# Four blocks of a position bias moved into the main run, and the first tokens' split moved apart from their transposition

## The chip, the cores and the metric

The kernel runs on one core of a Trainium2 chip. The metric is the device time of one execution in microseconds, as the median of several runs. The profile is one further execution, recorded by the hardware profiler.

## What is computed

Attention with a bias that a small MLP makes from positions, and then a mixture of experts (MoE) on the result. B = 8 batches, H = 8 heads, S = 576 positions, 64 columns a head; 4608 tokens of 512 columns, 8 experts, one expert for each token.

```python
scores = scale * np.matmul(q, k.transpose(0, 1, 3, 2))
x = (psi_rel / psi_i)[..., None]          # log1p(|i-j|) / log1p(max(i,1))
bias = np.maximum(x @ w1 + b1, 0.0) @ w2  # hidden 32, one value a head
scores = scores + bias.transpose(2, 0, 1)[None, :, :, :]
attn = softmax(scores); x = attn @ v      # tokens of 8 heads x 64
e_idx = np.argmax(x @ w_gate + modality_bias[modality_id], axis=1)
out[mask] = gate_w[mask, None] * (np.maximum(x[mask] @ w1[e], 0.0) @ w2[e])
```

## The kernel before, in words

The program has three stages. **The bias table** is made once. The 576 query rows are cut into 36 blocks of 16 rows. For each block four hidden tiles are made (L189 on ACT for the first of four, L191 on DVE for the others), TensorE multiplies them with w2 into a PSUM tile (`bias_out`, L199), and `bias_put` scales that into an output tile (L215 on ACT, L213 on DVE for the blocks in PUT_DVE) and issues its transfer on SP's queue. Blocks 0 to 31 are the main queries: each is one transfer of 288 KB into NBm (L218). NBm is read in four quarters, and quarter c holds blocks 8c to 8c + 7. Blocks 32 to 35 are the last 64 queries: each is four transfers of 72 KB into NBr (L223). `bias_table` runs blocks 0 to 31 in a loop with hooks for loads and transposes at given blocks; blocks 32 to 35 are generators (`bias_late`), which LATE steps at the head of the first units of pair 0: a first step makes the hidden tiles, a second the matmuls and the put.

**Attention** runs 32 pairs of heads, each in five units of queries: units 0 to 3 read the four quarters of NBm, unit 4 reads NBr. A unit is scores S (L400, TensorE), addition of the bias with row maximum (L414, DVE, `CUSTOM_DVE_ANT_0 Eb<-sps,NBm`), exponential (L429, ACT), transposes (L444), and the product with V (L486) three units later. ORDER writes the order of these steps by hand. In the following S(0,4) is the score step of pair 0's unit 4. A new pair's q, k, v come through SP's queue; V0 says where pair 0's V is loaded, (0, 1) being unit 1 of pair 0. Behind each transfer on SP the next waits in order; the transfers go round over eight semaphores, so that one is issued when the eighth before it has landed.

**MoE** runs tiles of 256 tokens. Weights and tokens are split into a high and a low part in fp32r: a cast on ACT makes the high part, a subtraction on DVE the low part (`wsplit` L1173, L1174; `wsplit_cols` L1181, L1182; tokens in `xprep`, L1195, L1196). `xprep` also copies gates and token numbers on POOL (L1190, L1191) and transposes the tokens on DVE (L1194). `phase1` multiplies with w1 (L1212), `phase2` with w2 (L1229), and `mo` (L1237) scales the result for the rows' transfer out. K = 5 tiles, the first ones, are dealt out from batches whose attention is done; `first_tiles` places the first tile's preparation among the last units of attention: the table `at` maps (place, unit) to what is done there.

Of the kernel before, what the change touches and what calls it, by code (L numbers as in the profile page):

```python
# [11 lines left out]
F32 = mybir.dt.float32  # L12
# [4 lines left out]
ALU = mybir.AluOpType  # L17
# [15 lines left out]
NDC = DM // P  # L33
NFC = F // P
TS = 256
# [5 lines left out]
NMAIN = P // 4  # L41
NBLK = S4 // 4
# [66 lines left out]
class Attn:  # L109
# [8 lines left out]

    ON_POOL, ON_DVE = (), (1,)


    LAG = 1
    PUT_DVE, ON_ACT2 = (21, 31, 34), ()
    TURN0, SPLIT0, QK1 = (4, 8), (6, 10), (9, 10, 11, 12, 13, 14, 15, 16)
    V0 = (0, 1)
    ROUTE = (6, 7, 8, 15, 16, 18)

    ROUTE_LATE = ((1, 1), (1, 2), (1, 3), (1, 4), (2, 0), (2, 1), (2, 3), (3, 0), (3, 1))  # L130

    LATE_HIDDEN = ((31, 0),)
    LATE = ((0, 1), (0, 0), (0, 2), (0, 1), (0, 3), (1, 2), (1, 3))

    def bias_setup(self):

# [43 lines left out]
    def bias_hidden(self, blk, cg, by):  # L180

        nc = self.nc
        s = bias_base(blk, cg)
        win = self.tg[:, X0 - s : X0 - s + S]
        c = self.shift[:, 4 * blk + cg : 4 * blk + cg + 1]
        h = next(h for h in self.bias_free if blk < NMAIN or not any(h is x for x in self.bias_main))
        self.bias_free = [x for x in self.bias_free if x is not h]
        if by == "act":
            nc.scalar.activation(h, win, AF.Relu, bias=c)  # L189
        else:  # L190
            (nc.gpsimd if by == "pool" else nc.vector).tensor_scalar(h, win, c, 0.0, op0=ALU.add, op1=ALU.max)  # L191
        return h
# [32 lines left out]
    def bias_table(self, hooks):  # L225

        ready = {}
        self.late = [self.bias_late(blk) for blk in range(NMAIN, NBLK)]

        def ahead(blk, cg):  # L230
            if blk < NMAIN and (blk, cg) not in ready:
                by = "pool" if cg == 3 and blk in self.ON_POOL else "act" if cg == 0 and blk not in self.ON_DVE or cg == 1 and blk in self.ON_ACT2 else "dve"
                ready[blk, cg] = self.bias_hidden(blk, cg, by)

        with self.tc.tile_pool(name="bps", bufs=3, space=PSUM) as pp:
            done = []
            for blk in range(NMAIN):
                ps = pp.tile([P, 1024], F32, tag="bps", name=f"bps{blk}")
                if blk + 3 in self.ON_POOL:
                    ahead(blk + 3, 3)  # L240
                for k in range(2):
                    if blk + k not in self.ON_DVE:
                        ahead(blk + k, 0)
                    if blk + k in self.ON_ACT2:
                        ahead(blk + k, 1)
                for cg in range(4):
                    ahead(blk, cg)
                    self.bias_out(cg, ready.pop((blk, cg)), (ps[:, 0:512], ps[:, 512:S]))
                for at, k in self.LATE_HIDDEN:
                    if at == blk:  # L250
                        next(self.late[k])
                if len(done) == self.LAG:
                    self.bias_put(*done.pop(0))
                done.append((blk, [(slice(0, S), ps[:, 0:S])]))
                for f in hooks.get(blk, ()):
                    f()
            for d in done:
                self.bias_put(*d)
# [299 lines left out]
    def attention(self):  # L558
        n_pair = self.n_pair
        tail = self.first_tiles() if self.K else {}  # L560
        for at in self.ROUTE_LATE:
            tail.setdefault(at, []).append(lambda: next(self.route, None))
        for u, k in self.LATE:
            tail.setdefault((0, u), []).append(lambda k=k: next(self.late[k], None))
        tail.setdefault(self.V0, []).append(lambda: self.load_v(0))
        bg = None
        for n in range(n_pair + 1):
            for u in range(5):
                for f in tail.get((n, u), ()):
                    f()  # L570
                if n == 1 and u == 0:
                    bg = self.blanks()
                if u == 4 and n > 0 and n % NP == 0:
                    assert not bg or all(k == len(x) for x, k in bg)
                    bg = self.route_steps(n // NP - 1)
                m, w = (n, u - 2) if u >= 2 else (n - 1, u + 3)
                scored = []
                for op in self.ORDER[u].split():
                    op, self.defer = op[0], int(op[1:] or 0)
                    if op in "aAbc":  # L580
                        self.flush(lambda x: x[0][0] in "er")
                    elif op == "X":
                        self.flush(lambda x: x[0][0] == "a")
                    self.held = [] if self.defer and op in "tTRAc" else None
                    if op in "SefC":
                        if n == n_pair:
                            continue
                        if op == "S":
                            scored = self.scores(n, u)
                        elif op == "C":  # L590
                            self.compact(n, u)
                        else:
                            self.exps(*scored["ef".index(op)])
                    elif op in "tT":
                        if 0 <= m < n_pair:
                            self.etrans(m, w, "tT".index(op))
                    elif op == "x":
                        if n > 0:
                            self.flush(lambda x: x[0][:2] == "av")
                            self.turn_x(n - 1)  # L600
                    elif op in "RaAbc":
                        if n > 0:
                            self.rtrans(n - 1) if op == "R" else self.av(n - 1, *divmod("aAbc".index(op), 2))
                    elif op in "qk01V":
                        if n + 1 < n_pair:
                            if op == "V":
                                self.load_v(n + 1)
                            elif op in "qk":
                                self.turn(n + 1, "qk".index(op))
                            else:  # L610
                                self.split(n + 1, int(op))
                    elif op == "L":
                        if n + 2 < n_pair:
                            self.load_qk(n + 2)
                    elif f := self.route_next(bg, "XB".index(op)):
                        f()
                    fresh, self.held = self.held or [], None
                    for x in self.waiting:
                        x[2] -= 1
                    self.flush(lambda x: x[2] <= 0)  # L620
                    self.waiting += fresh
                if 0 <= m < n_pair:
                    del self.E[m, w]
        self.flush(lambda x: True)
        self.bg = bg
# [555 lines left out]
        self.nc.scalar.copy(h, w)  # L1181
        self.nc.vector.tensor_tensor(l, w, h.bitcast(F32), op=ALU.subtract)  # L1182

    def xprep(self, t, x):

        nc = self.nc
        gx = self.gx[t % 2]
        for w in range(2):
            at = NDC * TS + 2 * w
            nc.gpsimd.tensor_copy(self.gate(t)[w], gx[:, at : at + 1])  # L1190
            nc.gpsimd.tensor_copy(self.ids_of(t)[w], gx[:, at + 1 : at + 2])  # L1191
        xh, xl = self.xh[t % 2], self.xl[t % 2]
        x = x.rearrange("p (c w) -> p c w", c=NDC)
        nc.vector.transpose(x, gx[:, 0 : NDC * TS].rearrange("p (a c i) -> p c a i", c=NDC, i=32))  # L1194
        nc.scalar.copy(xh, x)  # L1195
        nc.vector.tensor_tensor(xl, x, xh.bitcast(F32), op=ALU.subtract)  # L1196

    def phase1(self, t, before, beside):
        nc = self.nc
# [47 lines left out]
    def tile(self, t, beside=None, between=()):  # L1247

        parts = iter(range(NDC))
        beside = beside or (lambda: None)  # L1250
# [20 lines left out]
        self.load_new(t + 1, 1)  # L1271
        for c in range(NDC):
            self.wsplit(0, c)

        def middle(w):
            if w == 0 and t + 1 < self.T:
                self.xprep(t + 1, self.xt)
            beside()

        self.phase2(t, middle)  # L1280
        if t + 2 <= self.K:
            self.moe_rows(t + 2)
        if t + 2 <= self.T:
# [2 lines left out]
    def first_tiles(self):  # L1286

        nc = self.nc
        n = self.n_pair - NP
        at = {}  # L1290

        def add(pair, u, f):
            at.setdefault((n + pair, u), []).append(f)
# [5 lines left out]
        add(2, 4, lambda: self.load_rows(0))  # L1299
        for part, to in enumerate(((2, 4), (3, 1), (3, 3), (4, 0))):  # L1300
            add(*to, lambda part=part: self.load_part(1, part))
        add(4, 0, lambda: self.xprep(0, self.Eb[:, next(self.e_next)].rearrange("p h s -> p (h s)")[:, 0 : NDC * TS]))
        add(4, 3, lambda: self.wsplit_cols(0))
        return at

    def route_rest(self):
# [21 lines left out]
    def moe_rest(self, st):  # L1328
# [7 lines left out]
        if K == 0:  # L1336
            self.moe_load(0)
            self.load_new(0, 1)
            self.xprep(0, self.xt)
            self.moe_load(1)  # L1340
        first = self.sure - 2 * NT
        for t in range(K, self.sure):
# [150 lines left out]
```

## Time and profile before

| | us |
|---|---|
| median of 3 runs (1005.96 to 1006.64) | 1006.18 |
| the profiled execution's own time | 1007.5 |
| its span in the trace | 1005.4 |
| PE busy | 972.1 (97%) |
| DVE busy | 709.4 (71%) |
| ACT busy | 712.7 (71%) |
| POOL busy | 303.1 (30%) |

The span runs from the first to the last instruction that the trace holds; 2.1 us of the profiled time lie around it. PE is TensorE's matmul stream. The bias table takes the time to about 55 us, attention to about 573 us, MoE the rest. A row of a timeline gives its start, its duration (of a whole run of equal instructions where it ends in x2 or more), the engine, the line, and in square brackets how long the engine stood idle before it and which instruction released it.

### The profile page before, as it was taken

The page shows a single profiled execution, that of the slowest core. Times are in us where ns is not written, and L with a number is a line of the kernel's source. Part 1 is how long each engine was busy: PE and PEld are TensorE (multiplying, and loading weights), DVE is VectorE, ACT ScalarE, POOL GpSimd, SP SyncE. Part 2 cuts the span into 40 slices and gives each one's busy share as a digit, 9 for nine tenths or more (in the row PEclk, how much of TensorE's full clock was granted, in tenths as well). Part 3 has the DMA queues.
Part 4 walks back from the last instruction along what each step waited for, and adds up shares of the span by engine and source line. Part 5 has one row for each costly group of instructions (what it writes and reads, how often), then busy time and mean ns, then how long its engine had stood idle before and what let it go on. Part 6 is the DMA issues. An engine that isn't in the chain of part 4 may idle for free. (4 is left out here: it accounts for less than half of the span.)

```text
span 1005.4 us, 22478 instructions
## 1 busy us (share of the span) xinstructions
PE 972.1 (97%) x8110; PEld 762.4 (76%) x8110; DVE 709.4 (71%) x1441; ACT 712.7 (71%) x1366; POOL 303.1 (30%) x489
## 2 busy tenths in 40 slices
PE   7969999999999999999999899999999999999997
PEld 4547767767677676776667589889999998989896
DVE  8965768776777777777877677886666656565655
ACT  7977988888888888888888555455555555454554
POOL 1512433625426254262542513511111111111111
PEclk9998999999999999999999999999999999999999
DMA  6977755564655646546469430312117821162610
GB/s 163 194 166 152 196 104 116 109 131 101 128 108 105 134 100 120 119 101 133 94 121 212 128 112 32 96 48 64 43 43 190 271 64 54 61 195 68 186 43 24
DMA packets 327417, 116.34 MB, mean 116 GB/s; under 512 B 283247, under 2 KB 304111, under 8 KB 327299
## 3 DMA queue, kind: packets, MB, share of 16 engines
q1 hardware_dynamic: 321234, 95.80, 43.3%
q0 software_dynamic: 5920, 19.03, 5.4%
q8 instruction: 65, 1.06, 0.5%
q14 instruction: 54, 0.43, 0.2%
q10 hardware_dynamic: 144, 0.00, 0.0%
HBM read 144.34 MB, written 33.34 MB: 177 GB/s over the span
## 5 line engine op out<-in xcount | busy, mean ns | idle before, releaser
L414 DVE CUSTOM_DVE_ANT_0 Eb<-sps,NBm 128x576 f32<-128x576 f32 x256 | 183.6, 754 | 125.0 <-PE sps L400 57.1
L429 ACT ACTIVATE Eb<-Eb,mn 128x576 f32<-128x576 f32 x288 | 221.0, 769 | 13.6 <-DVE mn L414 12.6
L332 ACT ACTIVATE eT<-eps 128x512 f32<-128x512 f32 x256 | 148.9, 595 | 55.7 <-PE eps L444 54.8
L400 PE MATMUL sps<-QK 64*128 64x288 f32 (+1 forms) x1728 | 171.7, 310 | 7.5 <-DVE mn L414 7.0
L400 PEld LDWEIGHTS sps<-QK 64*128 64x128 f32 (+1 forms) x1728 | 134.3, 186 | 48.1 <-DVE mn L414 29.6
L1212 PE MATMUL p<-QK,w1hi 128*128 128x256 f32 x1136 | 161.8, 285 | 2.8 <-DVE QK L1196 2.2
L444 PE MATMUL eps<-idf,Eb 128*128 128x128 f32 x1024 | 149.6, 280 | 3.6 <-DVE eT L334 1.9
L1212 PEld LDWEIGHTS p<-QK,w1hi 128*128 128x128 f32 x1136 | 147.1, 191 | 7.3 <-DVE QK L1196 3.0
L486 PE MATMUL xps<-eT,vraw 128*64 128x288 f32 x1024 | 149.3, 416 | 0.0
L444 PEld LDWEIGHTS eps<-idf,Eb 128*128 128x128 f32 x1024 | 113.3, 141 | 37.5 <-issue 13.6
L1238 POOL DMA_INDIRECT out<-mo,idt x36 | 39.5, 1099 | 308.1 <-ACT mo L1237 252.4
L1214 ACT ACTIVATE hh<-p 128x512 fp32r<-128x512 f32 x72 | 43.1, 598 | 123.0 <-PE p L1212 116.7
L1215 DVE SCALAR_TENSOR_TENSOR hl<-p,hh 128x512 fp32r<-128x512 f32 x72 | 49.7, 691 | 101.6 <-ACT hh L1214 97.8
L1229 PE MATMUL p<-w2hi,hh 128*128 128x512 f32 x288 | 112.3, 390 | 0.0
L1229 PE MATMUL p<-w2hi,hl 128*128 128x512 f32 x288 | 112.3, 390 | 0.0
L434 POOL COPY rem<-Eb 128x128 f32<-128x128 f32 x128 | 37.0, 291 | 244.1 <-ACT Eb L429 238.3
L1174 DVE TENSOR_TENSOR w2lo<-NBm,w2hi 128x1024 fp32r<-128x1024 f32 x72 | 89.5, 1243 | 16.0 <-ACT w2hi L1173 15.7
L486 PEld LDWEIGHTS xps<-eT,vraw 128*64 128x64 f32 x1024 | 62.3, 136 | 39.9 <-issue 12.4
L1212 PE MATMUL p<-QK,w1lo 128*128 128x256 f32 x568 | 91.2, 283 | 0.0
L1174 DVE TENSOR_TENSOR w1lo<-NBm,w1hi 128x1024 fp32r<-128x1024 f32 x72 | 85.0, 1243 | 0.0
L1212 PEld LDWEIGHTS p<-QK,w1lo 128*128 128x128 f32 x568 | 78.3, 192 | 0.0
L1173 ACT CAST w2hi<-NBm 128x1024 fp32r<-128x1024 f32 x72 | 74.9, 1040 | 0.0
(219 smaller groups left out, 1451.0 us busy)
## 6 DMA issues: line engine op xcount, KB each, us to landing
NBm<-moe_w SPq DMA_DIRECT2D x84, 512.0 KB
NBm<-moe_w SPq DMA_DIRECT2D x42, 1024.0 KB
NBr<-xg SPq DMA_DIRECT2D x80, 128.0 KB
kraw<-k SPq DMA_DIRECT2D x128, 72.0 KB
xd<-xt SPq DMA_DIRECT2D x128, 72.0 KB
vraw<-v SPq DMA_DIRECT2D x64, 128.0 KB
NBm<-xTb SPq DMA_DIRECT2D x24, 288.0 KB
NBm<-moe_w SPq DMA_DIRECT2D x3, 2048.0 KB
```

Of the source, the lines that this page charges most:

```text
L332: self.nc.scalar.activation(out, ps, AF.Copy, scale=scale)
L400: nc.tensor.matmul(self.sps[h][:, half, 0:HS], QK[o, q, qs], QK[o, k, HS * half : HS * half + HS], start=i == 0, stop=i == 2, skip_group_c ...
L414: nc.vector.tensor_tensor_reduce(out=e.rearrange("p (t w) -> p t w", t=2), in0=self.sps[h][:, :, 0:HS], in1=nb.rearrange("p (t w) -> p t w ...
L429: self.nc.scalar.activation(e, e, AF.Exp, bias=mn, scale=-1.0, accum_out=sm)
L444: nc.tensor.transpose(ps[:, k, :], e[:, part, P * k : P * k + P], self.idf)
L486: nc.tensor.matmul(ps[out : out + 64, :], lhsT, rhs, tile_position=(row, out), skip_group_check=True, **kw)
L1173: self.nc.scalar.copy(h, w)
L1174: self.nc.vector.tensor_tensor(l, w, h.bitcast(F32), op=ALU.subtract)
L1212: nc.tensor.matmul(ps[:, a, :], w[:, c, fs], x[:, c, :], start=i == 0, stop=i == len(ops) - 1)
L1214: nc.scalar.activation(hh[:, sl, :], ps, AF.Relu)
L1215: nc.vector.scalar_tensor_tensor(hl[:, sl, :], ps, 0.0, hh[:, sl, :].bitcast(F32), op0=ALU.max, op1=ALU.subtract)
L1229: nc.tensor.matmul(ps, h[:, f, sl], m[:, f, :], start=i == 0, stop=i == len(ops) - 1)
```

## The change

Three things change. In the bias table, SEQ is the order of the main loop: the four blocks of the last 64 queries (32 to 35) stand in it behind main blocks 7, 11, 15 and 19, main blocks 29, 30 and 31 leave it, and the hooks go by place in SEQ. Blocks 29 to 31 are the late ones; LATE steps them behind the scores of units 0 and 1 instead of ahead of them. Their puts are on DVE (29 and 31) and ACT (30), and main block 21's stays on DVE. For the first tile, `xprep` is cut into `xturn` (POOL copies, transpose) and `xsplit` (cast, subtraction); `xturn` stays at (4, 0), `xsplit` goes to (4, 2), and the split of the first w1 columns moves from (4, 3) to (4, 2) behind it. In each later tile `xturn` stands between the second and the third part of the w1 split, and `xsplit` behind the fourth, ahead of phase 2; before, all of `xprep` stood behind the first half of phase 2.

```diff
-    PUT_DVE, ON_ACT2 = (21, 31, 34), ()
+    PUT_DVE = (21, 29, 31)
-    LATE_HIDDEN = ((31, 0),)
-    LATE = ((0, 1), (0, 0), (0, 2), (0, 1), (0, 3), (1, 2), (1, 3))
+    SEQ = (*range(8), 32, *range(8, 12), 33, *range(12, 16), 34, *range(16, 20), 35, *range(20, 29))
+    LATE = ((0, 0), (0, 1), (0, 2), (1, 1), (1, 2))
...
-        self.late = [self.bias_late(blk) for blk in range(NMAIN, NBLK)]
+        self.late_blocks = [blk for blk in range(NBLK) if blk not in seq]
+        self.late = [self.bias_late(blk) for blk in self.late_blocks]
...
-            for blk in range(NMAIN):
+            for at, blk in enumerate(seq):
...
-                for at, k in self.LATE_HIDDEN:
-                    if at == blk:
-                        next(self.late[k])
+                if at == len(seq) - 1:
+                    next(self.late[0])
...
-                for f in hooks.get(blk, ()):
+                for f in hooks.get(at, ()):
...
-        for u, k in self.LATE:
-            tail.setdefault((0, u), []).append(lambda k=k: next(self.late[k], None))
...
                             scored = self.scores(n, u)
+                            for _, j in (x for x in self.LATE if (n, x[0]) == (0, u)):
+                                next(self.late[j], None)
...
-    def xprep(self, t, x):
+    def xturn(self, t, x):
...
+        return x
+
+    def xsplit(self, t, x):
+
+        xh, xl = self.xh[t % 2], self.xl[t % 2]
+        self.nc.scalar.copy(xh, x)
+        self.nc.vector.tensor_tensor(xl, x, xh.bitcast(F32), op=ALU.subtract)
...
             self.wsplit(0, c)
-
-        def middle(w):
-            if w == 0 and t + 1 < self.T:
-                self.xprep(t + 1, self.xt)
-            beside()
-
-        self.phase2(t, middle)
+            if c == 1 and t + 1 < self.T:
+                x = self.xturn(t + 1, self.xt)
+        if t + 1 < self.T:
+            self.xsplit(t + 1, x)
+        self.phase2(t, lambda w: beside())
...
-        add(4, 0, lambda: self.xprep(0, self.Eb[:, next(self.e_next)].rearrange("p h s -> p (h s)")[:, 0 : NDC * TS]))
-        add(4, 3, lambda: self.wsplit_cols(0))
+        x0 = []
+        add(4, 0, lambda: x0.append(self.xturn(0, self.Eb[:, next(self.e_next)].rearrange("p h s -> p (h s)")[:, 0 : NDC * TS])))
+        add(4, 2, lambda: self.xsplit(0, x0[0]))
+        add(4, 2, lambda: self.wsplit_cols(0))
```

On SP's queue at the end of the bias loop, before (NBm and NBr are the bias tiles, vraw and vrem pair 0's V, one and quad two constants of the routing):

```order
L218 DMA NBm<-xt_73 16x8x576
L902 DMA one<-c_one 1x55
L923 DMA quad<-c_quad 128x1
L223 DMA NBr<-xTb_101 8x4x576 x16
L370 DMA vraw_810<-v 128x4x64 x2
L371 DMA vrem_118<-v 128x1x64
```

The same engine and place after the change, from the last of NBr's four groups on:

```order
L223 DMA NBr<-xt_73 8x4x576 x4
L218 DMA NBm<-xTb_101 16x8x576 x4
L218 DMA NBm<-xTb_100 16x8x576 x2
L218 DMA NBm<-xt_72 16x8x576
L218 DMA NBm<-xt_73 16x8x576
L218 DMA NBm<-xTb_101 16x8x576
L899 DMA one<-c_one 1x55
L920 DMA quad<-c_quad 128x1
L218 DMA NBm<-xTb_101 16x8x576
L367 DMA vraw_788<-v 128x4x64 x2
L368 DMA vrem_118<-v 128x1x64
L218 DMA NBm<-xTb_101 16x8x576 x2
```

The NBr transfers have gone forward in four groups (the last is shown), and of the main blocks one stands ahead of V's three transfers and two behind them.

On DVE at the start of pair 0, before (L191 makes hidden tiles; ISA Eb,mn is the bias addition of unit 0 and then 1, on two halves sps; L213 is a put):

```order
L191 TENSOR_SCALAR rT<-xTb_100,xrb_93 128x576
L191 TENSOR_SCALAR eT<-xTb_100,xrb_93 128x576 x6
L191 TENSOR_SCALAR rT<-xTb_100,xrb_93 128x576
L191 TENSOR_SCALAR eT<-xTb_100,xrb_93 128x576
L414 ISA Eb,mn_0_0_774<-sps_717,NBm 128x576
L414 ISA mn_0_0_774 128x1
L414 ISA Eb,mn_0_1_776<-sps_718,NBm 128x576
L414 ISA mn_0_1_776 128x1
L213 TENSOR_SCALAR xTb_101<-eps_719,xrb_93 128x512
L213 TENSOR_SCALAR xTb_101<-xps_82,xrb_93 128x64
L414 ISA Eb,mn_1_0_826<-sps_717,NBm 128x576
```

And after:

```order
L411 ISA Eb,mn_0_1_763<-sps_745,NBm 128x576
L411 ISA mn_0_1_763 128x1
L213 TENSOR_SCALAR xTb_101<-eps_747,xrb_93 128x512
L213 TENSOR_SCALAR xTb_101<-xps_82,xrb_93 128x64
L191 TENSOR_SCALAR eT<-xTb_100,xrb_93 128x576 x4
L191 TENSOR_SCALAR rT<-xTb_100,xrb_93 128x576
L191 TENSOR_SCALAR eT<-xTb_100,xrb_93 128x576
L411 ISA Eb,mn_1_0_804<-sps_744,NBm 128x576
L411 ISA mn_1_0_804 128x1
L411 ISA Eb,mn_1_1_806<-sps_745,NBm 128x576
L213 TENSOR_SCALAR xTb_101<-eps_747,xrb_93 128x512
```

The hidden tiles of the late blocks (six of them) stand now between the additions of units 0 and 1, and two puts instead of one follow additions.

On ACT at the end of attention, before (L429 is the last exponential, QK the first tile's split parts, eT, rT and xTb the copies of transposes and products out of PSUM):

```order
L429 ACTIVATE Eb,sums_7327<-Eb,mn_4_0_7494 128x576
L1195 CAST QK_76<-Eb 128x1024
L332 ACTIVATE eT<-eps_719 128x4x128
L332 ACTIVATE rT<-xps_82 128x512
L332 ACTIVATE eT<-eps_720 128x4x128
L332 ACTIVATE eT<-eps_719 128x4x2x64
L332 ACTIVATE rT<-eps_720 128x64
L332 ACTIVATE xTb_101<-xps_81 128x288
L1181 CAST QK_77<-NBm 128x1024
```

And after:

```order
L426 ACTIVATE Eb,sums_7327<-Eb,mn_4_0_7494 128x576
L329 ACTIVATE eT<-eps_746 128x4x128
L329 ACTIVATE rT<-xps_81 128x512
L329 ACTIVATE eT<-eps_747 128x4x128
L329 ACTIVATE eT<-eps_746 128x4x2x64
L329 ACTIVATE rT<-eps_747 128x64
L1196 CAST QK_76<-Eb 128x1024
L1178 CAST QK_77<-NBm 128x1024
L329 ACTIVATE xTb_101<-xps_82 128x288
```

The tokens' cast (L1195, now L1196) has gone behind the copies of the transposes, and the weights' cast ahead of the xTb copy.

## Rows read from the trace of the kernel before

**Rows 1.** The page, busy time by engine: us, share, instructions

```profile
PE 972.1 (97%) x8110; PEld 762.4 (76%) x8110; DVE 709.4 (71%) x1441; ACT 712.7 (71%) x1366; POOL 303.1 (30%) x489
```

**Rows 2.** PE's waits by line, whole run: us in total, times, longest

```profile
PE sps L400 <- DVE mn L414: 7.0, 5, 4.6
...
PE p L1212 <- DVE QK L1196: 2.2, 4, 1.1
...
PE xps L758 <- DVE xTb L334: 1.7, 1, 1.7
...
PE eps L450 <- ACT eT L332: 1.2, 1, 1.2
...
PE p L1212 <- ACT QK L1195: 0.7, 2, 0.5
```

**Rows 3.** Timeline of DVE, end of the bias loop and pair 0

```profile
53.51 0.82 DVE L213 TENSOR_SCALAR xt<-bps,xrb 128x576 f32<-128x576 f32 x1 [0.58 <-DMA NBm<-xt]
...
54.75 2.77 DVE L191 TENSOR_SCALAR eT<-xTb,xrb 128x576 f32<-128x576 f32 x6
...
58.30 0.75 DVE L414 CUSTOM_DVE_ANT_0 Eb<-sps,NBm 128x576 f32<-128x576 f32 x1
...
59.65 0.74 DVE L213 TENSOR_SCALAR xTb<-eps,xrb 128x512 f32<-128x512 f32 x1
...
66.27 0.76 DVE L414 CUSTOM_DVE_ANT_0 Eb<-sps,NBm 128x576 f32<-128x576 f32 x1 [0.44 <-issue]
...
73.68 0.76 DVE L414 CUSTOM_DVE_ANT_0 Eb<-sps,NBr 128x576 f32<-128x576 f32 x1 [4.78 <-DMA vraw<-v]
```

**Rows 4.** Timeline of PE, pair 0

```profile
56.85 1.06 PE L400 MATMUL sps<-QK 64*128 64x288 f32 x12
...
67.86 1.05 PE L400 MATMUL sps<-QK 128*128 128x288 f32 x6
68.83 1.09 PE L444 MATMUL eps<-idf,Eb 128*128 128x128 f32 x8
74.50 1.81 PE L400 MATMUL sps<-QK 64*128 64x288 f32 x12 [4.58 <-DVE mn L414]
```

**Rows 5.** SP's queue: its timeline, its waits (50 to 75), and NBr's issues (ns)

```profile
57.47 13.71 SPq L223 DMA_DIRECT2D NBr<-xTb  x16
...
SPq L223 <- DMA NBm<-xTb: 3.1, 4, 0.9
...
L223 SPq DMA_DIRECT2D NBr<-xTb x16: 588/588/698, 57.5 to 70.6; - x16
```

**Rows 6.** Windows: from:to, busy us by engine, PE's clock, DMA share, GB/s

```profile
56.00:60.00 4.00, 4.00 (x60) 2.22 (x51) 4.00 (x11) 3.77 (x9) 0.00 (x0) 1.00 1.05 221
...
65.00:70.00 5.00, 4.00 (x34) 3.35 (x33) 2.97 (x8) 5.00 (x12) 2.84 (x4) 1.00 0.37 109
...
74.00:80.00 6.00, 5.50 (x30) 4.89 (x30) 1.89 (x6) 3.47 (x9) 0.00 (x0) 0.50 0.74 125
```

**Rows 7.** Timelines of ACT, DVE and PE, end of attention

```profile
562.80 1.04 ACT L1195 CAST QK<-Eb 128x1024 fp32r<-128x1024 f32 x1 [0.48 <-DVE Eb L1194]
...
566.34 0.22 ACT L332 ACTIVATE rT<-eps 128x64 f32<-128x64 f32 x1 [0.53 <-PE eps L455]
...
569.32 2.33 DVE L1182 TENSOR_TENSOR QK<-NBm,QK 128x1024 fp32r<-128x1024 f32 x1 [3.22 <-ACT QK L1181]
...
572.64 1.04 PE L758 MATMUL xps<-xTb,wgb 128*32 128x512 f32 x2 [1.65 <-DVE xTb L334]
```

**Rows 8.** Timelines of DVE, ACT and PE, starts of the second and fourth MoE tile

```profile
594.49 1.25 DVE L1194 STREAM_TRANSPOSE xt<-NBr 128x1024 f32<-128x1024 f32 x1
596.85 1.22 DVE L1196 TENSOR_TENSOR QK<-xt,QK 128x1024 fp32r<-128x1024 f32 x1 [1.12 <-ACT QK L1195]
...
595.77 1.05 ACT L1195 CAST QK<-xt 128x1024 fp32r<-128x1024 f32 x1 [3.11 <-DVE xt L1194]
...
645.74 0.74 PE L1212 MATMUL p<-QK,w1hi 128*128 128x256 f32 x4 [1.05 <-DVE QK L1196]
```

More of the change, by code (lines that the diff above doesn't have):

```diff
@@ L117, in __init__ @@
         self.held, self.waiting, self.defer = None, [], 0
-    ON_POOL, ON_DVE = (), (1,)
+    ON_DVE = (1,)
     LAG = 1
-    PUT_DVE, ON_ACT2 = (21, 31, 34), ()
+    PUT_DVE = (21, 29, 31)
     TURN0, SPLIT0, QK1 = (4, 8), (6, 10), (9, 10, 11, 12, 13, 14, 15, 16)
@@ L185, in bias_hidden @@
         c = self.shift[:, 4 * blk + cg : 4 * blk + cg + 1]
-        h = next(h for h in self.bias_free if blk < NMAIN or not any(h is x for x in self.bias_main))
+        h = next(h for h in self.bias_free if blk not in self.late_blocks or not any(h is x for x in self.bias_main))
         self.bias_free = [x for x in self.bias_free if x is not h]
@@ L227, in bias_table @@
         ready = {}
-        self.late = [self.bias_late(blk) for blk in range(NMAIN, NBLK)]
+        seq = self.SEQ
+        self.late_blocks = [blk for blk in range(NBLK) if blk not in seq]
+        self.late = [self.bias_late(blk) for blk in self.late_blocks]
         def ahead(blk, cg):
-            if blk < NMAIN and (blk, cg) not in ready:
-                by = "pool" if cg == 3 and blk in self.ON_POOL else "act" if cg == 0 and blk not in self.ON_DVE or cg == 1 and blk in self.ON_ACT2 else "dve"
+            if (blk, cg) not in ready:
+                by = "act" if cg == 0 and blk not in self.ON_DVE else "dve"
                 ready[blk, cg] = self.bias_hidden(blk, cg, by)
@@ L236, in bias_table @@
             done = []
-            for blk in range(NMAIN):
+            for at, blk in enumerate(seq):
                 ps = pp.tile([P, 1024], F32, tag="bps", name=f"bps{blk}")
[L239 to L245, printed above, removed]
+                for b in seq[at : at + 2]:
+                    if b not in self.ON_DVE:
+                        ahead(b, 0)
                 for cg in range(4):
@@ L1191, in xprep @@
             nc.gpsimd.tensor_copy(self.ids_of(t)[w], gx[:, at + 1 : at + 2])
-        xh, xl = self.xh[t % 2], self.xl[t % 2]
         x = x.rearrange("p (c w) -> p c w", c=NDC)
         nc.vector.transpose(x, gx[:, 0 : NDC * TS].rearrange("p (a c i) -> p c a i", c=NDC, i=32))
-        nc.scalar.copy(xh, x)
-        nc.vector.tensor_tensor(xl, x, xh.bitcast(F32), op=ALU.subtract)
+        return x
[3 more added lines that the diff above has]
+        self.nc.vector.tensor_tensor(xl, x, xh.bitcast(F32), op=ALU.subtract)
     def phase1(self, t, before, beside):
@@ L1338, in moe_rest @@
             self.load_new(0, 1)
-            self.xprep(0, self.xt)
+            self.xsplit(0, self.xturn(0, self.xt))
             self.moe_load(1)
```

## The prediction

> **What bounds the kernel now.** I read the busy table first: PE has work in 97% of the span [rows 1], so time is won or lost only where PE stands idle or runs at a lower clock. The list of PE's waits then names the places [rows 2]. The largest is 7.0 us before score matmuls (L400), 4.6 of it in one wait; the reader is to see next that p L1212 (first matmuls of a MoE tile) waits 2.2 + 0.7 us and that waits of 1.2 and 1.7 us (eps L450, xps L758) belong to the passage from the last attention pair to the first tile.
>
> The 4.6 us lie in pair 0. DVE starts the fourth unit's bias addition at 66.27 and the fifth's, which reads NBr, only at 73.68, after 4.78 us idle [rows 3]. The profile names a V load as the releaser; the instruction reads NBr and not V, and the last of the 16 NBr transfers is issued just before the V loads, so I take NBr. SP needs 13.71 us from 57.47 on to issue them [rows 5]. PE finishes its last transposes at 69.92 and starts S(1,0) at 74.50 [rows 4]. The windows show the second loss: 1.00 granted until 70, and after the idle stretch 0.50, the 1.2 GHz level, from 74 to 80 with PE 5.50 us busy [rows 6]. Work of 5.50 us at half speed is 2.75 us at full speed, so 2.75 us are lost there.
>
> Later units and pairs show no such wait; tiles from the fifth on have no wait on L1212 (the six in rows 2 all lie before 670 us). What is saved at any of the three places reaches the end, since PE works nearly without a gap behind them.
>
> **The change part by part.** *A, bias table.* No work is added or removed: 36 blocks before and after. The main loop makes 33 instead of 32, so it ends about one block later. A block costs three DVE operations (six took 2.77 us, so 0.46 each) and a little more, about 1.4 us [rows 3]. The loop's last copy ended at 53.51 + 0.82 = 54.33; it will end near 55.7. Two blocks' output matmuls stood ahead of S(0,0), which therefore began at 56.85 [rows 4]; now none does. S(0,0) starts near 55.9 and the first addition near 57.0, against 58.30 (bounds 56.6 and 58.4: the copy buffers may stall the loop).
>
> From there DVE's new order can be added up. Two additions of one unit with their reads take 59.65 - 58.30 = 1.35. The copy of block 29 takes 0.74 for 512 of its 576 columns, near 1.0 in its two pieces. Then six hidden rows, 2.8; unit 1's additions, 1.35; the copy of block 31, 1.0. That puts the last copy's end at 57.0 + 7.5 = 64.5. Two transposes of 0.8 and unit 2's 1.35 put unit 3's addition at 67.4, about 1.1 later than before, if its bias is there.
>
> Is it? Unit 3 reads all of NBm's last quarter, so blocks 29 to 31; the stall can't vanish, it only moves from unit 4 to unit 3 unless block 31 lands by 67.4. The last NBr was issued at 57.47 + 13.71 = 71.18 less its own 0.59 [rows 5], and its reader began at 73.68, 3.1 us behind. A main block has four times the bytes; at 221 GB/s [rows 6] its 294,912 bytes need 1.33 us against about 0.3, so 4.1 us: the reader can't begin before 64.5 + 4.1 = 68.6. That is the lower bound of t_a, the start of unit 3's addition. It holds if the queues are empty. They aren't: the 16 engines are full (share 1.05) to about 60 us. By then the kernel before has moved 32 main blocks and half a block of NBr. The changed one must move 36 blocks and V's 288 KB before or with block 31, so 37 - 32.5 = 4.5 blocks more, 4.5 x 1.33 = 6.0 us: data end at 66.0 if fed without a gap, reader 3.1 later at 69.1. The other end is set by the NBr transfers now inside the full stretch. Alone they ran at 109 GB/s [rows 6], 2.7 us per block instead of 1.33. If the other engines idle meanwhile, four blocks cost 4 x 1.37 = 5.5 us: reader at 74.6. SP adds to that: its NBr issues waited 3.1 us for earlier NBm transfers [rows 5], and blocks 30 and 31 now stand behind block 29's and three V transfers on that queue. I take t_a = 71.4, a little under the middle of 68.6 and 74.6, because the nearest row (share 1.05 with mixed traffic) speaks for engines that are kept fed.
>
> *The Trainium skill, "DMA: Bandwidth & Descriptors", section "Why a DMA increments its semaphore by 16 and not by 1", says that a transfer is spread over the largest number of engines, up to 16, that divides the slowest dimension of both sides; by that rule an 8x4x576 transfer uses 8 engines, which agrees with the 109 GB/s against 221 here. It speaks against this change, and would put t_a towards 74.6, if the same 8 are always chosen.*
>
> What follows t_a: PE restarts 0.82 later with S(0,4) (as S(1,0) did, 73.68 to 74.50), and has S(0,4) and the transposes of unit 2 still to do, 69.92 - 67.86 = 2.06 us, which before lay ahead of the stall. So S(1,0) stands at t_a + 2.88 against 74.50 before, and A = t_a - 71.6, if the clock falls as it did and the slow stretch is as long. PE will be idle from about 68.5 to 72.2, 3.7 us against 4.58; I take it that the clock falls again. A = -0.2 us. If it stays up, 2.75 more are gained: A = t_a - 74.35.
>
> The four-queue issues moved into the loop cost SP 16 x 0.59 = 9.4 us there; SP has no other work than one 0.6 us issue per 1.4 us, so it keeps up (33 x 0.6 + 9.4 in 45 us).
>
> *B, first tile's tokens.* ACT's cast of the first tile's tokens (1.04, at 562.80) stood ahead of the copy that PE then waited 1.2 for [rows 2, 7]; without it ACT is free, so that wait (eps L450 in rows 2) goes: -1.24. Then DVE's w1 remainder (2.33 at 569.32, with POOL beside it) held up two copies that PE waited 1.65 for, to 572.64. These copies ended 1.0 behind it, at 572.64. Now ACT's two casts begin behind the rT copy, which ended at 566.56 and comes 1.24 earlier: 565.3. DVE's two subtractions start one cast later, at 566.4, and at 2.3 for one (POOL beside it) and 1.2 for the other [rows 8] end at 569.9; with the copies PE resumes at 570.9, 1.7 ahead of 572.64, the 1.24 contained. Bounds: both subtractions at 2.3 give 572.0 (-0.6), both out of the way give all of 1.24 + 1.65 = -2.9. I take -1.7.
>
> *C, MoE tile.* Before, DVE did four w1 parts, the transpose (1.25), then waited 1.12 for ACT's cast and did the subtraction (1.22) [rows 8]. With the transpose after two parts the cast runs under the other two; the subtraction ends 1.1 earlier. PE's six waits, of which the longest stands in [rows 8], were 0.35, 0.25, 0.45 + 1.05 and 0.21 + 0.52 at four tile starts, 2.83 in all (2.2 + 0.7 in rows 2). The first, second and fourth (0.35, 0.25, 0.73) are under 1.1 and go; of the third's 1.50, 0.4 stays. The sum is -2.4. The moved cast delays mo, whose PSUM bank PE needs later, by up to 1.05; I keep 0.2 for that: -2.2, bounds -1.5 and -2.8. From the fifth tile on PE waits for neither, so the same edit gives nothing.
>
> Sum: -0.2 - 1.7 - 2.2 = -4.1. The profiled run took 1007.5 (span 1005.4 and 2.1 around it), 1.3 over the median; its counterpart after would be 1003.4, and against the median 1006.18 - 4.1 = 1002.1.
>
> **The rivals.** (1) *The stall shrinks and the clock stays up.* Block 31 lands early, t_a 69.1: A = 69.1 - 74.35 = -5.2, sum -9.1, 997.1. For it: the engines are kept fed, and the idle is shorter than the 4.58 that ended in the fall. Against it: three V transfers stand ahead of block 31's.
> (2) *The NBr transfers clog the full stretch*: uneven engines delay both the loop (its copies wait for output buffers) and blocks 29 to 31. At t_a = 74.6, A = +3.0, sum -0.9: 1005.3, no change. It decides for slower when A passes 3.9 + 2.0 = 5.9, so from t_a = 77.5 on, with the loop's end 3 us later still: 1008.2 or more. For it: PE's restart depends on one late transfer. Against it: SP has time, and 77.5 is beyond the bound.
> (3) *B and C are hidden*: another wait takes the place of the removed ones (the PSUM bank held by mo, the copies behind the subtractions). With B -0.6, C -0.3 and A -0.2, 1005.1. Against it: ACT was free for 3.1 us ahead of the cast that moves [rows 8].
>
> **How the numbers follow.** The forecast (stall moved to unit 3, clock falls, B and C gained) has 0.45, with its own range 999.5 to 1004. Rival 1 has 0.28, rival 2's no-change end 0.12, its slower end 0.07, rival 3 0.08. A measurement tells about 0.2%, 2.0 us: faster is under 1004.2, slower over 1008.2. Faster takes 0.43 of the forecast's and all of rival 1's, 0.71; same 0.02 + 0.12 + 0.08 = 0.22; slower 0.07. Low end: A at -5.2, B -1.7 and C at its bound of -2.8 is 996.5. High end: A at +3.0 with B -0.6 and C -1.5 is 1007.1.
>
> **What would show it.** PE's longest wait before L400 stands before S(0,4), at about 72, and is released by unit 3's addition; unit 4's has no wait of its own. The granted clock after it is 0.50 for about 6 us (forecast) or 1.00 (rival 1). The wait L450 <- ACT is gone, L758's is under 0.5, and L1212's sum is under 0.7. The loop's last copy ends near 55.7; past 58 speaks for rival 2. I am wrong if unit 3 starts before 69 or after 74, or if L1212 waits from the fifth tile on.

## The result: slower by half a per cent

The changed kernel takes 1011.36 us in the median (1010.43 to 1012.69, 5 runs) against 1006.15 for the kernel before: ratio 1.0053, interval 1.0039 to 1.0066, or 5.2 us more. A gain of 4 us was forecast, and the time lies above the range (996.5 to 1007.1). The profiled run took 1010.47 with a span of 1008.7. Between the two profiled runs there are only 3.0 us, because the one before lay 1.3 over its median and this one 0.9 under its own.

The span can be cut at four points that both traces have. Each difference is that of the starts or ends of the same instruction.

| place | before | after | moved | since the line above |
|---|---|---|---|---|
| first copy of block 0 (ACT) | 9.30 | 9.80 | +0.50 | +0.50, nothing of the change lies ahead of it |
| last attention unit's transposes after the wait for eT (PE) | 561.62 | 567.41 | +5.79 | +5.29, bias table |
| first tile's first matmul (PE) | 573.62 | 576.35 | +2.73 | -3.06, first tile's tokens |
| PE's last matmul ends | 998.13 | 999.82 | +1.69 | -1.04, MoE tiles |
| end of the span | 1005.4 | 1008.7 | +3.3 | +1.6, behind PE's last matmul |

So the first tile's part gained more than forecast (3.06 against 1.7). The MoE tiles' part gained half of its 2.2 up to PE's end, less than its lower bound of 1.5, and gave more than that back behind PE's last matmul. The bias table lost over 5 us where -0.2 was written.

PE's waits of the changed kernel (us in total, times, longest), to be set against [rows 2]:

```profile
PE sps L397 <- ACT xTb L215: 5.4, 1, 5.4
...
PE sps L397 <- DVE mn L411: 3.6, 4, 2.1
PE p L1213 <- DVE QK L1197: 2.4, 2, 2.0
```

The long wait before a score matmul isn't the one of [rows 4]. It stands before S(0,0) and is released by ACT's copy of a bias block (L215), that is, by the end of the bias loop. The waits L450 (1.2) and L758 (1.7) of before are gone. L1213, which was L1212, has two waits for DVE and ACT instead of six, 2.4 us instead of 2.9; 2.0 of them stand at the fourth tile's start.

The same place on ACT and DVE (timelines, columns as in [rows 3]; ACT's last two copies of the loop, then DVE):

```profile
59.85 0.74 ACT L215 ACTIVATE xt<-bps,xrb 128x576 f32<-128x576 f32 x1 [3.29 <-DMA NBr<-xt]
60.99 0.74 ACT L215 ACTIVATE xTb<-bps,xrb 128x576 f32<-128x576 f32 x1 [0.40 <-DMA NBm<-xTb]
```

```profile
46.48 0.82 DVE L213 TENSOR_SCALAR xTb<-bps,xrb 128x576 f32<-128x576 f32 x1 [1.97 <-DMA NBm<-xTb]
...
63.73 0.76 DVE L411 CUSTOM_DVE_ANT_0 Eb<-sps,NBm 128x576 f32<-128x576 f32 x1 [7.34 <-ACT eT L189]
...
77.91 0.76 DVE L411 CUSTOM_DVE_ANT_0 Eb<-sps,NBm 128x576 f32<-128x576 f32 x1 [3.61 <-DMA qraw<-q]
...
79.96 0.76 DVE L411 CUSTOM_DVE_ANT_0 Eb<-sps,NBr 128x576 f32<-128x576 f32 x1
```

The copies wait for output tiles that transfers still read: 3.29 us for an NBr transfer, 1.97 for an NBm one (the experiments below set apart what these two come from). The loop's last copy ends at 61.73, not at 55.7; unit 0's first addition starts at 63.73, not at 57.0; unit 3's at 77.91, not at 71.4. Unit 4's no longer waits.

The windows (columns as in [rows 6]; of before, 30 to 50) show what the transfers did meanwhile. Before:

```profile
30.00:40.00 10.00, 10.00 (x127) 5.53 (x122) 10.00 (x23) 10.00 (x16) 10.00 (x1) 1.00 1.11 194
40.00:50.00 10.00, 10.00 (x115) 5.03 (x114) 10.00 (x24) 8.87 (x14) 0.16 (x1) 1.00 1.05 207
```

After:

```profile
30.00:40.00 10.00, 10.00 (x129) 5.58 (x124) 10.00 (x24) 10.00 (x17) 10.00 (x1) 1.00 0.90 155
40.00:50.00 10.00, 8.99 (x99) 3.86 (x94) 8.03 (x19) 6.82 (x11) 5.79 (x1) 1.00 0.77 179
50.00:60.00 10.00, 6.15 (x75) 2.90 (x71) 6.38 (x20) 6.54 (x11) 0.00 (x0) 0.97 1.01 180
60.00:70.00 10.00, 8.22 (x70) 4.57 (x71) 5.64 (x15) 5.07 (x10) 0.29 (x1) 0.69 1.03 210
```

The DMA engines were not clogged between 30 and 50, they were short of work: share 0.90 and 0.77 where it had been 1.11 and 1.05. Too few transfers had been issued.

The granted clock fell twice where it had fallen once: behind the 5.4 us idle before S(0,0) (0.69 as a mean over 60 to 70), and again from 80 on, behind the wait for unit 3's addition. PE's rows and the windows there:

```profile
61.78 1.81 PE L397 MATMUL sps<-QK 64*128 64x288 f32 x12 [5.39 <-ACT xTb L215]
...
78.73 1.05 PE L397 MATMUL sps<-QK 128*128 128x288 f32 x6 [2.06 <-DVE mn L411]
...
82.01 1.66 PE L397 MATMUL sps<-QK 64*128 64x288 f32 x12
```

```profile
80.00:82.00 2.00, 1.89 (x8) 1.56 (x8) 0.72 (x2) 1.42 (x4) 0.29 (x1) 0.50 0.74 153
82.00:83.00 1.00, 1.00 (x9) 0.99 (x10) 0.00 (x0) 0.88 (x2) 0.00 (x0) 0.50 0.50 93
83.00:84.00 1.00, 1.00 (x12) 0.84 (x9) 0.16 (x1) 0.47 (x2) 0.00 (x0) 0.82 0.81 137
```

The second slow stretch is shorter than the one of before: it is over by 84, less than 4 us behind its start, where the other lasted about 6 us [rows 6].

SP's queue says why. The kernel before, all issues from 26.65 to 33.47 us (start, duration, transfer):

```profile
26.65 0.58 SPq L355 DMA_DIRECT2D qraw<-q  x1
27.36 1.72 SPq L218 DMA_DIRECT2D NBm<-xTb  x1
29.13 0.58 SPq L360 DMA_DIRECT2D kraw<-k  x1
29.81 0.53 SPq L218 DMA_DIRECT2D NBm<-xTb  x1
30.39 0.59 SPq L357 DMA_DIRECT2D qraw<-q  x1
31.04 0.53 SPq L358 DMA_DIRECT2D qraw<-q  x1
31.66 0.54 SPq L218 DMA_DIRECT2D NBm<-xTb  x1
32.24 0.59 SPq L360 DMA_DIRECT2D kraw<-k  x1
32.93 0.54 SPq L218 DMA_DIRECT2D NBm<-xt  x1
```

The changed kernel, from one NBr group to the second main block behind it:

```profile
30.44 0.53 SPq L218 DMA_DIRECT2D NBm<-xTb  x1
31.02 0.59 SPq L354 DMA_DIRECT2D qraw<-q  x1
31.65 0.51 SPq L355 DMA_DIRECT2D qraw<-q  x1
32.26 2.76 SPq L223 DMA_DIRECT2D NBr<-xTb  x4
35.06 0.44 SPq L357 DMA_DIRECT2D kraw<-k  x1
36.16 0.56 SPq L218 DMA_DIRECT2D NBm<-xt  x1
37.16 0.32 SPq L354 DMA_DIRECT2D qraw<-q  x1
37.55 0.48 SPq L355 DMA_DIRECT2D qraw<-q  x1
38.07 0.66 SPq L664 DMA_DIRECT2D rev<-c_rev  x1
38.84 0.57 SPq L218 DMA_DIRECT2D NBm<-xt  x1
```

Before, SP had gaps of 0.05 to 0.13 us between issues here: q and k loads stand between the main blocks, and five of the nine issues are not main blocks. A group of four holds the queue for 2.76 us, and the main blocks, one in 1.3 to 2.5 us before, come at 30.44, 36.16 and 38.84. Between 30 and 50 us SP's waits for earlier transfers to land come to 1.2 us in all, so what the groups take from the queue is in the main the time of their issues.

The tail, POOL's last two row transfers (timelines). Before:

```profile
994.32 1.13 POOL L1238 DMA_INDIRECT out<-mo,idt  x1 [15.98 <-ACT mo L1237]
...
999.76 0.98 POOL L1238 DMA_INDIRECT out<-mo,idt  x1 [3.77 <-ACT mo L1237]
```

After:

```profile
997.62 1.78 POOL L1239 DMA_INDIRECT out<-mo,idt  x1 [13.88 <-ACT mo L1238]
1002.75 0.99 POOL L1239 DMA_INDIRECT out<-mo,idt  x1 [3.34 <-DMA out<-mo,idt]
```

In the last tile the scaling of the first half (mo) now stands behind the next tile's token cast on ACT, which waits for the transposition; so its rows leave late, at 997.62 instead of 994.32, and the second transfer waits for the first to land. It had waited only for its own data.

### The profile page after: what moved, and what is told of

Its sections match the earlier page's. It is cut to its first block, busy times and chain, and to the rows that moved or that the text cites. A ratio compares the mean times of both kernels' runs of the same rounds, so it can differ in the third digit from the quotient of the medians.

```text
span 1008.7 us, 22462 instructions
## 1 busy us (share of the span) xinstructions
PE 974.1 (97%) x8110; PEld 763.1 (76%) x8110; DVE 706.2 (70%) x1442; ACT 710.5 (70%) x1364; POOL 324.1 (32%) x489
## 5 line engine op out<-in xcount | busy, mean ns | idle before, releaser
L1213 PE MATMUL p<-QK,w1hi 128*128 128x256 f32 x1136 | 161.2, 285 | 2.4 <-DVE QK L1197 2.4
L1213 PEld LDWEIGHTS p<-QK,w1hi 128*128 128x128 f32 x1136 | 147.2, 192 | 5.8 <-DVE QK L1197 2.8
L1216 DVE SCALAR_TENSOR_TENSOR hl<-p,hh 128x512 fp32r<-128x512 f32 x72 | 49.7, 690 | 118.2 <-ACT hh L1215 118.0
L1239 POOL DMA_INDIRECT out<-mo,idt x36 | 48.0, 1334 | 257.6 <-ACT mo L1238 171.4
L1213 PE MATMUL p<-QK,w1lo 128*128 128x256 f32 x568 | 91.3, 283 | 0.0
L1213 PEld LDWEIGHTS p<-QK,w1lo 128*128 128x128 f32 x568 | 78.4, 192 | 0.0
```

What stands on the lines that cost most here:

```text
L1213: nc.tensor.matmul(ps[:, a, :], w[:, c, fs], x[:, c, :], start=i == 0, stop=i == len(ops) - 1)
L1216: nc.vector.scalar_tensor_tensor(hl[:, sl, :], ps, 0.0, hh[:, sl, :].bitcast(F32), op0=ALU.max, op1=ALU.subtract)
L1239: nc.gpsimd.indirect_dma_start(out=self.out, out_offset=IndirectOffsetOnAxis(ap=ids, axis=0), in_=o, in_offset=None, bounds_check=self.n_t ...
```

## The experiments

**The three parts alone.** Each kernel is the one before with one part of the change. The bias table alone (`SEQ`, `LATE`, `PUT_DVE` and what reads them, as in the diff above):

> The kernel before with the bias-table part alone (order of blocks, late blocks 29 to 31); first tile and MoE tiles as before. Theory 1, from the two traces (the attention drain's wait for eT moved from 561.62 to 567.41, of which 0.5 to 1.0 is a later start of the loads): this part costs +4.8 to +5.8 us by itself, so 1011 to 1012. Rival (the prediction's sum): the stall only changes its unit and the part costs -0.2, within 1004 to 1008; then the loss lies in the MoE part. The trace should show the main loop's copies waiting for output tiles that NBr transfers still read.

Measured: 1012.98 us, ratio 1.0067 (1.0048 to 1.0087). The part costs 6.7 us by itself; the rival is out.

The first tile's part alone (`xsplit` and `wsplit_cols(0)` at (4, 2)):

> The kernel before with the first tile's part alone. Theory: from the two traces (first tile's matmul 12.00 behind the drain's eT wait before, 8.94 after) -3.1 us, so 1003.1. The prediction's step had -1.7 with bounds -0.6 and -2.9. Rival: part of the gain is lost again by the end and the time is within 1 us of before.

Measured: 1003.72, ratio 0.9980 (0.9969 to 0.9991), a gain of 2.0 (by the ratio) to 2.7 us (by the medians). The list of PE's waits has neither L450 nor L758 any more.

The MoE tile's part alone:

> The kernel before with the MoE tile's part alone. Theory: PE's end comes 1.0 us earlier, but in the last tile the first half's scaling now stands behind the next tile's cast and low parts of ACT's queue, the first of the two row transfers leaves 2 to 3 us later, the second waits for it, and the tail grows by 1.6: in sum +0.6, 1006.8. The prediction's step: -2.2, 1004.0, with an unchanged tail of 7.3 us from PE's last matmul to the span's end.

Measured: 1006.65, ratio 1.0003 (0.9991 to 1.0014): nothing is left of the gain. PE's last matmul ends at 994.88, and the span at 1003.2, 8.3 us behind it; before it was 7.3. (Only this 8.3 can be set against before, not the 994.88: the profiled run took 1004.97, the least of its ten and 1.7 under their median.) PE's waits at the tile starts fell from 2.9 to 2.1, and 1.0 more behind PE's end makes +0.2 of it, against +0.3 measured.

The same with the cast behind the first half's scaling:

```diff
-        if t + 1 < self.T:
-            self.xsplit(t + 1, x)
-        self.phase2(t, lambda w: beside())
+        def middle(w):
+            if w == 0 and t + 1 < self.T:
+                self.xsplit(t + 1, x)
+            beside()
+
+        self.phase2(t, middle)
```

> As c_only, but the cast and subtraction of the next tile's tokens stand behind the first half's scaling again; only the transposition stays between the second and third part of the w1 split. If the tail's loss comes from the order of scaling and cast on ACT, the tail is back at 7.3 us and the time is 1.6 us under c_only's: 1004.0 to 1005.2. If the loss comes from the transposition's place, the time is c_only's.

Measured: 1004.12, ratio 0.9982 (0.9971 to 0.9992). The tail is back at 7.2 us (994.72 to 1001.9), and the wait before L1216, as L1212 is called there, falls to 1.1 us from 2.9. These two, -0.1 and -1.8, make the whole of the gain (1.8 by the ratio). So the transposition's new place is good, and what c_only lost again it lost by the order of cast and scaling, the one thing in which the two kernels differ. The tiles' own rows, PE's waits in c_only and in c_mo_first:

```profile
PE p L1216 <- DVE QK L1200: 2.1, 1, 2.1
```

```profile
PE p L1216 <- DVE QK L1200: 1.1, 2, 0.8
```

In c_only the one wait left is that at the fourth tile's start. ACT's w1 casts wait there for weights:

```profile
632.32 3.90 ACT L1173 CAST w1hi<-NBm 128x1024 fp32r<-128x1024 f32 x4 [1.94 <-DMA NBm<-moe_w]
```

Before, these casts waited for nothing. In c_only ACT comes to them at 630.38 and meets its weights' transfer; in c_mo_first it comes at 631.89 and doesn't wait. So in c_only part of the gain of the earlier starts is given back here.

**What of the bias table costs the time.** Two theories: half-used engines (E) or SP's queue (N). First the transfers' shape, four of 16 partitions each:

```diff
-                    r = 64 * par + 2 * (blk - NMAIN) + a
-                    nc.sync.dma_start(self.NBr[r : 64 * par + 64 : GS, :, :], o[64 * a + par : 64 * a + 64 : 2, :])
+                    r = 2 * (blk - NMAIN) + a
+                    nc.sync.dma_start(self.NBr[r : P : GS, 2 * par : 2 * par + 2, :], o[64 * a + par : 64 * a + 64 : 2, :])
```

> As a_only, but each of the four transfers of a last-queries block is cut to 16 partitions x 2 heads x 576 instead of 8 x 4 x 576: same bytes, same number of transfers, other places in NBr (so the last queries' bias is another one). Theory E (a transfer over 8 rows loads half of the DMA engines and the main blocks behind it wait for that half): the loop's last copy comes back to 56 to 58 us (61.7 after the change), unit 3's addition to 70 to 72, time 1004 to 1008. Theory N (four transfers take four of the eight places in SP's round, and the queue then waits for landings): as a_only, 1011 to 1013.

Measured: 1010.80, ratio 1.0043 (1.0026 to 1.0060), some 2.4 us under a_only, in intervals that overlap. The loop's last copy ends at 59.83 (62.74 in a_only, 61.73 in the changed kernel, whose loop is the same, so two profiles of one loop differ by 1.0 here), unit 3's addition starts at 76.59 (79.07). ACT's longest wait for an NBr transfer is 0.9 (4.08 and 3.29 there), while DVE's wait for an NBm one stays at 2.4, and the DMA share at 0.87 and 0.74 between 30 and 50. So the long wait for NBr went with the eight rows; the want of work for the DMA engines stayed without them. Between the two theories' forecasts: E has a share, but not the larger one.

Then one transfer a block:

```diff
-            for par in range(2):
-                for a in range(2):
-                    ...
+            r = blk - NMAIN
+            nc.sync.dma_start(self.NBr[r : P : 4, :, :], o)
```

> As a_only, but a last-queries block goes out in one transfer of 32 x 4 x 576 (288 KB like a main block's; other places in NBr, so the last queries' bias is another one). Both theories E and N take the loop's last copy back to 56 to 58 us and give 1003 to 1007. If a_16eng is already there, the number of transfers costs under 1 us; if a_16eng is as slow as a_only and this is fast, it is the number. If this one is slow too (1010 or more), the cause is the late place of main blocks 29 to 31 alone.

Measured: 1006.73, ratio 1.0005 (0.9994 to 1.0016). From a_16eng to here it is 3.8 us, and 12 issues fewer. DVE's wait for an NBm transfer falls to 1.0, and the DMA share is back at 1.01 and 0.97. So N is right about the number of transfers; that they cost places in SP's round, as N words it, isn't what the rows show, since SP waits little for landings (the 1.2 us above): they cost issue time. ACT's last copy of the loop and DVE's addition of unit 3:

```profile
55.66 0.74 ACT L215 ACTIVATE xTb<-bps,xrb 128x576 f32<-128x576 f32 x1 [0.73 <-DMA NBm<-xTb]
```

```profile
72.18 0.76 DVE L409 CUSTOM_DVE_ANT_0 Eb<-sps,NBm 128x576 f32<-128x576 f32 x1 [4.64 <-DMA NBm<-xTb]
```

The copy ends at 56.40 (55.7 forecast), the addition starts at 72.18 (71.4 forecast), and the time comes out 0.5 above before by the ratio, where A = t_a - 71.6 gives 0.6; the interval of -0.6 to 1.6 can't tell that from nothing. With one issue a block the prediction's sum for this part fits.

The groups' place in the loop:

```diff
-    SEQ = (*range(8), 32, *range(8, 12), 33, *range(12, 16), 34, *range(16, 20), 35, *range(20, 29))
+    SEQ = (0, 1, 32, 2, 33, 3, 34, 4, 35, *range(5, 29))
```

> As a_only, but the last queries' four blocks stand in the main run behind main blocks 1 to 4 instead of 7, 11, 15 and 19, where the DMA engines were not yet full before (share 0.66 between 10 and 20 us). Theory E or N: the clogging drains before the full stretch, the loop ends near 56 to 58, the stall stands before unit 3 with its addition near 71, 1005 to 1008. Rival: any place in the loop costs the same, since the total of 37 block loads bounds it: 1011 to 1013.

Measured: 1016.51, ratio 1.0087 (1.0065 to 1.0110), the slowest of all. (A quarter of block 32's hidden values is made from positions that are not scaled yet, so its bias is another one; the work is the same.) The expectation under both theories was wrong: it took the early stretch to have room because the DMA share there was 0.66. DMA had room, SP had not: its issues stand back to back from 15.1 to 31 us, with three main blocks among them up to 26 us. The share fell to 0.42 between 10 and 20 and main blocks came later from the start.

Then the converse, without any change of places: the kernel before, with four main blocks cut into four transfers each.

```diff
-            nc.sync.dma_start(self.NBm[k:P:GS, H * c : H * c + H, :], o)
+            cut = 4 if blk in (8, 12, 16, 20) else 1
+            for j in range(cut):
+                nc.sync.dma_start(self.NBm[k:P:GS, H * c + j : H * c + H : cut, :], o[j:P:cut, :])
```

> The kernel before with one edit: main blocks 8, 12, 16 and 20 go out in four transfers of 16 x 2 x 576 each instead of one; same bytes, same engines, same order, the last queries' blocks late as before. Theory N (SP's queue is full between 20 and 45 us, each further issue of 0.6 us holds up the main blocks behind it, and the full DMA engines then run dry): 12 more issues delay the loop's last copy by 2 to 4 us from 54.3, and the whole by 2.5 to 4 us, 1009 to 1010.5. Rival (the loss came from the last queries' places and from half-used engines alone): within 1 us of before.

Measured: 1008.29, ratio 1.0021 (1.0011 to 1.0032). The loop's last copy moved by 3.7, as N said, and what came of it in the time, 2.1, is under the forecast 2.5 to 4: DVE's rows show the stall before unit 4 shrinking from 4.78 to 2.37 at the same time, and the slow stretch moving (mean clock 0.81 over 60 to 70, 1.00 over 70 to 80).

```profile
57.18 0.82 DVE L213 TENSOR_SCALAR xt<-bps,xrb 128x576 f32<-128x576 f32 x1 [3.61 <-DMA NBm<-xt]
...
77.21 0.76 DVE L416 CUSTOM_DVE_ANT_0 Eb<-sps,NBr 128x576 f32<-128x576 f32 x1 [2.37 <-DMA vraw<-v]
```

Last, pair 0's V behind blocks 30 and 31 (`load_v(0)` called after the late steps of unit 1 instead of ahead of it):

> As a_only, but pair 0's V (three transfers, 288 KB) is issued behind main blocks 30 and 31 instead of ahead of them. If V's place sets when block 31 lands, unit 3's addition comes 1.4 to 2 us earlier than a_only's 79.07 and the time is 1011 to 1011.6. If put 31 itself is the last to come (it ended at 72.5), the time stays within 0.7 of a_only's 1013.0.

Measured: 1011.04, ratio 1.0044 (1.0029 to 1.0059); unit 3's addition starts at 77.37. The forecast was met. V's place is worth about 2 us, in intervals that overlap (a_only's is 1.0048 to 1.0087). The copy of block 31 ends at 72.8 here and at 72.5 in a_only, and yet the addition starts 1.7 earlier; so block 31's landing, and not its copy, sets the wait.

**Better versions.** The changed kernel with the cast behind the scaling (same diff as c_mo_first):

> The changed kernel with one edit: the cast and subtraction of the next tile's tokens stand behind the first half's scaling again, as in c_mo_first. Theory (tail): 2.5 us under the changed kernel's 1011.4, so 1008.9, with the span's end 7.3 us behind PE's last matmul.

Measured: 1007.97, ratio 1.0018 (1.0008 to 1.0028): 3.4 us less than the changed kernel, in another series of runs, where 2.5 was expected; the wait before L1213 is 0.4 us there instead of 2.4. The span ends 7.0 us behind PE's last matmul (998.96 to 1006.0).

The kernel before with half of NBr's transfers on GpSimd's queue:

```diff
-                    nc.sync.dma_start(self.NBr[r : 64 * par + 64 : GS, :, :], o[64 * a + par : 64 * a + 64 : 2, :])
+                    (nc.gpsimd if a else nc.sync).dma_start(self.NBr[r : 64 * par + 64 : GS, :, :], o[64 * a + par : 64 * a + 64 : 2, :])
```

> The kernel before with one edit: half of NBr's 16 transfers on GpSimd's queue. From bc_pool (996.2) less b_only's 2.7 and c_mo_first's 2.3 the edit alone is worth 5.2 us: 1001. The addition of unit 4 should start near 71.2 instead of 73.7, and the granted clock should stay at 1.00 from 70 to 80 us.

Measured: 1000.58, ratio 0.9940 (0.9921 to 0.9959). The five runs are 1000.25 to 1002.15 and one of 1005.36; the profile is of the last, and the two points on the trace failed there: the addition of unit 4 starts at 72.12 and the clock's mean over 70 to 80 is 0.66. Over the whole run the mean clock is 0.995 in it and 0.997 to 0.999 in the other four.

All that gained, together: the table as before, NBr on two queues, the first tile's part, and c_mo_first's part.

> The table as before (last queries' blocks late), first tile's part and the MoE part of c_mo_first, and half of NBr's 16 transfers issued on GpSimd's queue instead of SP's. Without the queue's change b_only's -2.7 and c_mo_first's -2.3 give 1001.4. Theory S (SP's 16 issues of 0.6 to 1.4 us, 13.7 us in all, set the stall before unit 4): SP is through about 5 us sooner, the wait of 4.6 falls under 1 and the 1.2 GHz stretch behind it goes: -5 to -7 more, 994.5 to 996.5. Rival (the 8 engines at 109 GB/s set it, 1.18 MB take 10.8 us): -1 to -3 more, 998.5 to 1000.5.

Measured: 996.17, ratio 0.9897 (0.9880 to 0.9914), 10 us under the kernel before and 15 under the changed one. DVE's and PE's rows at the place of [rows 3] and [rows 4], and the window:

```profile
71.19 0.76 DVE L414 CUSTOM_DVE_ANT_0 Eb<-sps,NBr 128x576 f32<-128x576 f32 x1 [2.09 <-DMA qraw<-q]
```

```profile
72.01 1.05 PE L400 MATMUL sps<-QK 64*128 64x288 f32 x12 [1.90 <-DVE mn L414]
```

```profile
70.00:80.00 10.00, 8.10 (x84) 5.79 (x83) 4.42 (x12) 7.89 (x19) 0.78 (x5) 1.00 0.68 116
```

The wait is 1.90 instead of 4.58, not under 1 as expected; S(1,0) runs at full clock (1.05 for twelve matmuls, 1.81 before), and the 2.75 us of the slow stretch are saved too. That the second queue gains because SP is through earlier fits these rows, but no run sets it apart from another cause, a second way into the DMA engines, say.

## Why the prediction was wrong

**The bias table: the step that failed is the one on SP.** It said that "SP has no other work than one 0.6 us issue per 1.4 us, so it keeps up (33 x 0.6 + 9.4 in 45 us)". SP's rows of 26 to 33 us before the change, which aren't among the rows that the prediction rests on, show a queue without gaps to speak of: main blocks are less than half of its issues there. Over the whole loop the sum fits; in the stretch where the first groups were put it doesn't. SP, which the sum had at nothing, has a price: with 12 issues fewer the loop's last copy ends at 56.40 instead of 59.83 (a_16eng to a_one). From there the chain is: groups hold SP, main blocks are issued late, output tiles come free late, the copies wait (3.29 and 1.97 us), the loop ends at 61.73 and not at 55.7. b_split4 shows the first link by itself (12 more issues, last copy 3.7 later), a_one its removal. The shape has a part of its own, the 3.29, as a_16eng shows.

The one price that the prediction did put on these transfers, 109 GB/s and so 5.5 us for four blocks, was SP's as well. In the window of 65 to 70 [rows 6] SP issues one NBr transfer in 0.64 us, without a gap; at 72 KB each that is 115 GB/s, and the DMA share is 0.37. The 109 is the rate at which SP issued, so it says nothing of how many engines such a transfer uses, and "agrees" was too much.

**t_a.** The upper bound of 74.6 was none. It let the slow NBr transfers delay block 31's data, but kept its copy's end at 64.5, as if the loop did not feel them; the measured copy came about 7 us later. The wait did move from unit 4 to unit 3, the stall didn't vanish, and V's place ahead of blocks 30 and 31 cost about 2. A = t_a - 71.6 gives +6.3 for 77.91, against +5.29 in the table above (5.79 from the span's start), but this is partly luck: S(1,0) starts 4.10 behind t_a (82.01), not 2.88, and the slow stretch behind it is shorter than before, not as long; the two errors nearly cancel. For a_one the formula gives +0.6 and measured +0.5. So the way from t_a to the time was near enough, and t_a was wrong because the loop's end was.

**Rival 2** had the right mechanism in its first sentence, the copies that wait for output buffers, and put its point at t_a = 77.5 and at a loop 3 us later than 58. It got 0.07 because of "SP has time", the same error. It also named uneven engines as the cause; a_16eng puts these at the smaller part, about 2.4 of 6.2 us (the ratios of a_only, a_16eng and a_one). The Trainium skill ("DMA: Bandwidth & Descriptors", "Why a DMA increments its semaphore by 16 and not by 1") says that a transfer goes over the largest number of engines, up to 16, that divides the slowest dimension of both sides, so an 8x4x576 one over 8 and a_16eng's over 16. The runs point that way, 1010.80 us against 1012.98 and the loop's last copy at 59.83 against 62.74, though the times' intervals overlap.

**Rival 1** and the forecast shared the error. The clock did fall behind unit 3's wait, as the forecast took it, and also behind the wait for the loop's end, a place that neither the forecast nor a rival named.

**Rival 3** came true in part: at the fourth tile another wait, for weights, took the place of the removed ones.

**The first tile: right, a little small.** -1.7 was written with a bound of -2.9; -3.06 stands in the trace and 2 to 2.7 in the timed runs. The term that was too large is the subtraction at 2.3: both took 1.2. Before, a POOL operation of 1.03 us stood beside the slow one (569.53); after, POOL's stand at 569.43 and 575.72 and none beside either (571.93, 573.08).

**The MoE tile: one term was missing.** The waits at PE behaved as written, except at the fourth start, where 2.0 us stand instead of 0.73, because the weights were not there. The delay of mo was seen ("delays mo ... by up to 1.05") and charged with 0.2 for its PSUM bank. What else follows mo, the last tile's row transfers, was not looked at: it cost 1.6 us behind PE's last matmul. The prediction's sentence that what is saved "reaches the end" holds for PE's end, not for the span's.

**The sum by parts:** +6.7 (bias table), -2.4 (first tile, middle of 2 to 2.7), +0.2 (MoE tiles) make +4.5, against +5.2 with an interval of 3.9 to 6.6.

## What to carry to other kernels

A queue that issues transfers is an engine like the others: before moving issues into a stretch, read that queue's own rows there, not its average over the loop. A step off the critical path that is moved ahead of another on the same engine delays that other one in the last iteration too, where nothing hides it. And where one transfer is split into four by its layout, try a second queue before trying another place.

## What the runs showed that was not expected

The DMA share can fall because of too many small issues: 0.77 over 40 to 50 with groups of four in the loop, 0.97 with one issue a block, 1.05 before. In bc_pool the half of NBr's transfers on GpSimd's queue took 5.6 to 7.9 us from issue to landing and still cut the stall from 4.78 to 2.09; SP was through at 66.6 instead of 71.2. And the granted clock after a wait at the same place differs from run to run: with 2.88 us idle on DVE the profiled run of n_pool fell to a mean of 0.66 over 70 to 80, while the other four runs of that kernel were 3 to 5 us faster, at a mean clock of 0.997 to 0.999 over the whole run where it had 0.995. Where in those runs the clock stayed up can't be seen, since they have no profile.
